# More buffers for the block sums of the experts' weights, and other numbers of pairs per stretch

## The chip, the cores and the metric

The kernel runs on one core of a Trainium2 chip. The metric is the device time of one execution in microseconds (us). TensorE (PE) multiplies matrices, VectorE (DVE) and ScalarE (ACT) work elementwise, SyncE (SP) issues nearly all transfers, and 16 DMA engines carry them out.

## The reference

Three layers follow each other on 2304 tokens (4 batches of 576) of width 512:

```python
kv = einsum('bhsd,bhse->bhde', k, v);  out = einsum('bhsd,bhde->bhse', q, kv)
x = out / sqrt(mean(out * out, -1) + 1e-6) * g_norm          # linear attention
h = x @ w_in;  x = (h * clip(h + 3, 0, 6) / 6) @ w_out       # first feed-forward, d_ff 2048
p = domain_probs / (domain_probs.sum(-1) + 1e-9)
out = sum over 4 experts e of p[:, e] * (relu(x @ w1[e]) @ w2[e])     # d_ff 1024 each
```

All is float32. The kernel gets that accuracy from pairs: an operand is split in a high part, rounded to float32r, and the low rest, and three products (high x high, high x low, low x high) stand for one.

## The kernel before

*Stages.* The attention comes first (to about 70 us). Then the first feed-forward, up to about 473 us. Then the experts, to the end.

*First feed-forward.* The tokens lie in five blocks `t` (four of 512, block 4 of 256). The 2048 hidden columns are 16 weight tiles of 128, taken in five units `u` of 1, 2, 3, 4 and 6 tiles (`UNITS1`). A step `n` is one (u, t, f); there are 80. In step n the 12 matmuls of `ff_in` (lines 360 to 362, `ph`) make a hidden tile, ACT and DVE apply the nonlinearity and split it into `gH` and `gL` (lines 373 to 377), and the 12 matmuls of `ff_out` of step n - 3 (line 395) add into four PSUM banks `po`. There are six such banks. After the last tile of a unit `ff_end` drains the four banks into `acc[t]`: ACT and DVE copy in unit 0, DVE adds later (line 413). `acc` tiles come from pool `accp`, five slots of 8 KB a partition, so block 4, half as long, fills half a slot.

*Conversion of weight tiles.* `convert(n)` turns raw 64-bit weights of tile n into `W`, in one of eight slots w0 to w7 of pool `wp`: tile n goes to w((6 + n) mod 8). It works on four buffers of 512 words a partition in pool `cvp` (tags x, a, and r with two). ACT (lines 166, 167), DVE (169 to 180) and again ACT (182, high part) and DVE (184, low part) make half 0, which `ff_in` needs, and then half 1, for `ff_out`. `load_raw` (line 152) fetches halves into `rawp`, three buffers. Conversions are paced by `pull(n)`, a tile only after the last use of the tile eight before it.

*Block sums.* The experts use a product scheme of seven instead of eight block products. It needs sums of blocks of `w1` and `w2`, which are split in high and low and put into DRAM (`dwin`, `dtw`, `dwo`) for later. This is `blocks(k, h)`: k is one of 16 pairs of hidden tiles, h is 0 for `w1` and 1 for `w2`. It takes 6 pieces: two of sums on DVE (line 676) and four calls of `keep` with an ACT copy (line 662), a DVE subtraction (line 663) and the transfers on SP (lines 666, 670, and 672 for the last two k). Each gets eight buffers `tb` from `new()`, in turn out of the four buffers of `cvp`:

```python
tag = ("x", "a", "r", "r")[turns[0] % 4]
```

A buffer can be written again when its transfer to DRAM has landed. The raw block (`rawt`, 512 KB) comes by lines 636 and 640 into `rawp`, and the next load is issued after the last piece of the one before.

*Stretches.* 24 calls of `blocks` are done within the first feed-forward, in three stretches between conversions, since both use `cvp` and `rawp`: from step 23 (after tile 9), from step 37 (after tile 13) and from step 54 (after tile 15). `BLOCKS` lists for each stretch the last tile converted, how many raw blocks are loaded in advance and the pairs; `second(n)` advances so many pieces a step.

*The start of the experts.* From step 69 on a list `ahead` of 20 jobs is worked off beside the steps: splits and differences of `acc` (`build(0)`) and the conversions `convert_in(0)`, `convert_in(1)` of the first two pairs into `win`, whose raw tiles (`load1`, line 779) lie in w6 and w7. TensorE first uses `win[0]` at line 1032, and goes on at line 885.

*Order.* Up to step 4 the order on the engines is written by hand. From there on a planner that runs when the program is built puts the instructions of each engine in order, with its own estimates of durations and the text order as priority. An engine works its list strictly in order.

Of the kernel before, what the change touches and what calls it, by code (L numbers as in the profile page):

```python
# [8 lines left out]
F32 = mybir.dt.float32  # L9
F32R = mybir.dt.float32r  # L10
# [7 lines left out]
def kernel(  # L18
# [22 lines left out]
    P = 128  # L41
    KD = DM // P
    TB = 512
# [29 lines left out]
    accp = ctx.enter_context(tc.tile_pool(name="accp", bufs=NB))  # L73
# [3 lines left out]
    wp = wst.enter_context(tc.tile_pool(name="wp", bufs=1, side="right"))  # L77
# [4 lines left out]
    cvp = early.enter_context(tc.tile_pool(name="cvp", bufs=1, side="right"))  # L82
# [7 lines left out]
    NG = CJ * 2  # L90
# [46 lines left out]
    def load_raw():  # L137
        if not todo:
            return
        nn, h = todo.pop(0)  # L140
        u, f = ftiles[nn]
        g = sum(UNITS1[:u]) + f
        r = rawp.tile([P, KD * P, 2], U32, tag="raw", name="raw")
        if h == 0:
            dst = r.rearrange("p (c f) w -> p c (f w)", c=KD)
            src = moe_w_in.bitcast(U32)[:, 2 * g * P:2 * (g + 1) * P].rearrange("(c p) f -> p c f", p=P)
        else:
            dst = r.rearrange("p (c f) w -> p c (f w)", c=2)
            src = moe_w_out.bitcast(U32)[g * P:(g + 1) * P, :].rearrange("p (c f) -> p c f", c=2)
        n = dst.shape[1] // 2  # L150
        for c in (slice(0, 2 * n),) if done[0] or len(flow) < 8 else (slice(0, n), slice(n, 2 * n)):
            paced(nc.sync.dma_start(out=dst[:, c], in_=src[:, c]))
        raw[nn, h] = r
# [189 lines left out]


    acc = {}
    gt = {}
    po_t = {}

# [53 lines left out]
    def ff_end(u, t):  # L402
        ps = po_t.pop((u, t))
        n = BLK[t][1]
        if u == 0:
            acc[t] = accp.tile([P, KD, n], F32, tag="acc", name="acc1")
        for o, p in enumerate(ps):
            if u == 0 and o < KD - 1:
                nc.scalar.activation(out=acc[t][:, o, :], in_=p, func=AF.Copy)
            elif u == 0:  # L410
                nc.vector.tensor_copy(out=acc[t][:, o, :], in_=p)
            else:
                nc.vector.tensor_tensor(out=acc[t][:, o, :], in0=p, in1=acc[t][:, o, :], op=ALU.add)  # L413
# [11 lines left out]
    def step(n):  # L425
        if n < NI:
            ff_in(*items[n])
        if n >= NB + LAG:
            for _ in ff_out(*items[n - LAG]):
                pass  # L430

        if 0 <= n - LAG + 1 < NI:
            u, t, _ = items[n - LAG + 1]
            rate = RATE[u] // (1 + (u == 3 and t == NB - 1))
            budget[0] = min(budget[0] + rate, rate)
            pull(n)
# [180 lines left out]
    TC = DM // 2  # L617
    experts = [(e, j) for e in range(E) for j in range(FP)]
    NG = len(experts) // 2
# [7 lines left out]
    def load_rawt():  # L627
        if not wanted:
            return
        k, h = wanted.pop(0)  # L630
        e, j = experts[k]
        f = 2 * j * P
        r = rawp.tile([P, 4, 2 * P], F32, tag="raw", name="rawt")
        rawt[k, h] = r
        if h:
            nc.sync.dma_start(
                out=r.rearrange("p (f c) d -> p f (c d)", f=2),
                in_=moe2_w2[e, f:f + 2 * P, :].rearrange("(f p) d -> p f d", p=P))
        else:
            nc.sync.dma_start(out=r, in_=moe2_w1[e, :, f:f + 2 * P].rearrange("(c p) f -> p c f", p=P))  # L640

    turns = [0]

    def blocks(k, h):

        r = rawt[k, h]
        last = k - 2 * NG + 2 if h else -1

        def new():
            tag = ("x", "a", "r", "r")[turns[0] % 4]  # L650
            turns[0] += 1
            return cvp.tile([P, 2, TC], F32R, tag=tag, bufs=2 if tag == "r" else 1, name="tb")

        def keep(m, src, low, n=2):
            high = new()
            low = low if low is not None else new()
            hi, lo = high[:, :n], low[:, :n]
            if src is None:
                src = lo.bitcast(F32)
            elif not h:  # L660
                hi, lo = (x.rearrange("p m (c f) -> p (m c) f", c=2) for x in (hi, lo))
            nc.scalar.activation(out=hi, in_=src, func=AF.Copy)
            nc.vector.tensor_tensor(out=lo, in0=src, in1=hi.bitcast(F32), op=ALU.subtract)  # L663
            for y, x in ((0, high), (1, low)):
                if not h:
                    nc.sync.dma_start(
                        out=dwin[k][:, y, m:m + n].rearrange("p m c f -> p m (c f)"), in_=x[:, :n].bitcast(F32))
                    continue
                c = min(n, 7 - m) if m else 1
                nc.sync.dma_start(out=dtw[k // 2][:, m:m + c, k % 2, y], in_=x[:, :c].bitcast(F32))  # L670
                if last >= 0 and m < 2:
                    nc.sync.dma_start(
                        out=dwo[last][:, int(m > 0), y].rearrange("p (c d) -> p c d", c=2), in_=x.bitcast(F32))

        def sub(out, a, b, op=ALU.subtract):
            nc.vector.tensor_tensor(out=out, in0=a, in1=b, op=op)  # L676

        odd = new()
        od = odd.bitcast(F32)
        if h:  # L680
            sub(od, r[:, 1::2], r[:, 0:2])
        else:
            q = r.rearrange("p c (i f) -> p i c f", i=2)
            a11, a12, a21, a22 = (q[:, i, 2 * c:2 * c + 2] for i in range(2) for c in range(2))
            o4 = od.rearrange("p m (c f) -> p m c f", c=2)
            sub(o4[:, 0], a21, a22, ALU.add)
            sub(o4[:, 1], o4[:, 0], a11)
        yield
        even = new()
        ev = even.bitcast(F32)  # L690
        if h:
            sub(ev[:, 0], r[:, 3], od[:, 0])
            sub(ev[:, 1], r[:, 2], ev[:, 0])
        else:
            e4 = ev.rearrange("p m (c f) -> p m c f", c=2)
            sub(e4[:, 0], a11, a21)
            sub(e4[:, 1], a12, o4[:, 1])
        yield
        keep(3, None, odd)
        yield  # L700
        keep(5, None, even)
        yield
        if h:
            keep(1, r[:, 2:4], None)
        else:
            keep(0, q[:, 0], None)
        yield
        if not h:
            keep(2, a22, None, 1)
        elif last >= 0:  # L710
            keep(0, r[:, 0:2], None)
        else:
            keep(0, r[:, 0:1], None, 1)
        rawt.pop((k, h))
        load_rawt()
        yield

    stream = []
    BLOCKS = {
        23: (9, 2, [(2, 0), (4, 0), (6, 0), (8, 0)]),  # L720
        37: (13, 2, [(k, 1) for k in range(9)] + [(10, 0)]),
        54: (15, 3, [(k, 1) for k in range(9, 2 * NG)] + [(12, 0), (14, 0), (15, 0)]),
    }

    def second(n):
        if n in BLOCKS:
            tile, deep, todo2 = BLOCKS[n]
            assert not stream and not rawt and cv[0] == tile + 1
            assert tile + 1 == len(ftiles) or todo[0] == (tile + 1, 1)
            wanted.extend(todo2)  # L730
            for _ in range(deep):
                load_rawt()
            stream.extend(x for k in todo2 for x in [blocks(*k)] * 6)
        for _ in range(5 if 23 < n < 29 or 54 < n < 68 else 6 if 37 < n < 48 else 0):
            if stream:
                next(stream.pop(0))
        if n in (28, 29, 48, 49):
            load_raw()

    N3 = start[NU1 - 1, 0] + 3 * UF[NU1 - 1]  # L740
    for n in range(NB, N3 + 1):
        step(n)
        second(n)
# [153 lines left out]
    ahead += [run(convert_in(0, sums))] * 6 + [run(convert_in(1, sums))] * 6  # L897
    for n in range(N3 + 1, NI):
        step(n)
        for _ in range(2):  # L900
            if ahead:
                ahead.pop(0)()
    for x in ahead + [first["7-"], first[7], first[3]]:
# [199 lines left out]
    for jj, i, f in order:  # L1103
        t, o = divmod(i * P, TH)
# [37 lines left out]
```

## Time and profile before

| | us |
|---|---|
| median of 3 runs | 1190.9 (1189.87 to 1192.04) |
| profiled execution, its own time | 1192.36 |
| its span, first to last instruction | 1190.5 |
| TensorE busy | 1164.2 (98%) |
| DVE busy | 871.6 (73%) |
| ACT busy | 591.1 (50%) |

Times in the trace count from the first instruction. Matmuls overlap in their pipeline, so an interval between starts tells more than a duration. The granted clock is TensorE's, as a share of 2.4 GHz.

### The profile page before, as it was taken

How to read it: one execution, taken by the hardware profiler on the slowest of the kernel's cores; microseconds unless marked ns; L12 is line 12 of the kernel's file. 1: busy time of each engine (PE TensorE's matmuls, PEld its weight loads, DVE VectorE, ACT ScalarE, POOL GpSimd, SP SyncE). 2: the span in 40 equal slices, each digit the busy share in tenths (PEclk: the TensorE clock that was granted, in tenths of full speed). 3: DMA queues.
4: the chain of work that ended last, by engine and by line, in shares of the span. 5: the costliest groups of instructions: out<-in, count | busy, mean ns of one | idle time of the engine just before them, and what ended most of it. 6: DMA issues, size and time to landing. Idle time of an engine off the chain costs nothing.

```text
span 1190.5 us, 20959 instructions
## 1 busy us (share of the span) xinstructions
PE 1164.2 (98%) x8244; PEld 1087.4 (91%) x8244; DVE 871.6 (73%) x1572; ACT 591.1 (50%) x1052; POOL 7.6 (1%) x15
## 2 busy tenths in 40 slices
PE   8999999999959999999999999999999999999998
PEld 6788888888848879999999999999999999999997
DVE  5889987976777796677777696666666866666663
ACT  5877544644454553544444454444444544444441
POOL 1100000000000000000000000000000000000000
PEclk9999999999989999999999999999999999999999
DMA  8723255467868856477777889777777897777721
GB/s 308 244 76 122 89 181 192 140 209 242 274 217 266 273 218 229 161 260 268 265 266 272 309 289 328 255 251 248 251 248 249 296 327 249 251 247 249 252 103 53
DMA packets 105686, 274.60 MB, mean 231 GB/s; under 512 B 9460, under 2 KB 56564, under 8 KB 99188
## 3 DMA queue, kind: packets, MB, share of 16 engines
q1 hardware_dynamic: 105104, 272.48, 66.2%
q8 instruction: 65, 1.06, 0.4%
q10 hardware_dynamic: 484, 0.79, 0.2%
q14 instruction: 33, 0.27, 0.1%
HBM read 207.69 MB, written 65.54 MB: 230 GB/s over the span
## 4 chain that ended last, share of the span: by engine, by line
PE 84%; DMA 7%; DVE 6%; ACT 1%; issue 1%; SPq 0%; DVEq 0%; ACTq 0%
PE slot L1011 29%; PE qa L885 15%; PE qb L885 15%; PE po L395 11%; PE ph L360 4%; PE ph L362 4%; PE ph L361 4%; DMA dtw<-tb 3%; PE slot L1106 1%; DMA vin<-in_v_dram 1%; DVE tb L663 1%; DVE tb L676 1%; DMA kin<-in_k_dram 1%; DMA dwin<-tb 1%; DMA qin<-in_q_dram 1%
## 5 line engine op out<-in xcount | busy, mean ns | idle before, releaser
L1011 PE MATMUL slot<-tt,so 128*128 128x256 f32 x2898 | 372.0, 282 | 0.0
L1011 PEld LDWEIGHTS slot<-tt,so 128*128 128x128 f32 x2898 | 365.7, 190 | 0.3 <-ACT slot L1018 0.2
L865 DVE SCALAR_TENSOR_TENSOR acc<-slot,prob,acc 128x256 f32<-128x256 f32 (+1 forms) x384 | 163.8, 482 | 112.7 <-PE slot L1011 103.8
L885 PE MATMUL qa<-xs,win 128*128 128x384 f32 x1008 | 202.4, 335 | 0.2 <-ACT qa L947 0.2
L885 PE MATMUL qb<-xs,win 128*128 128x384 f32 x1008 | 202.4, 335 | 0.0
L395 PE MATMUL po<-gH,w 128*128 128x512 f32 (+1 forms) x632 | 191.0, 368 | 1.7 <-DVE acc L413 1.6
L784 DVE TENSOR_TENSOR so<-ar,so 128x768 fp32r<-128x768 f32 x142 | 135.3, 954 | 57.3 <-ACT so L783 56.2
L885 PEld LDWEIGHTS qa<-xs,win 128*128 128x128 f32 x1008 | 173.8, 188 | 0.6 <-ACT qa L947 0.5
L885 PEld LDWEIGHTS qb<-xs,win 128*128 128x128 f32 x1008 | 172.7, 189 | 0.1
L783 ACT ACTIVATE so<-ar 128x768 fp32r<-128x768 f32 x142 | 119.4, 842 | 37.7 <-PE slot L1011 32.3
L395 PEld LDWEIGHTS po<-gH,w 128*128 128x128 f32 x632 | 115.7, 188 | 22.5 <-DVE acc L413 2.0
L360 PE MATMUL ph<-xh,w 128*128 128x512 f32 (+1 forms) x320 | 119.5, 374 | 12.8 <-ACT w L182 12.7
L361 PE MATMUL ph<-xl,w 128*128 128x512 f32 (+1 forms) x320 | 118.4, 370 | 0.0
L362 PE MATMUL ph<-xh,w 128*128 128x512 f32 (+1 forms) x320 | 118.2, 370 | 0.0
L395 PE MATMUL po<-gL,w 128*128 128x512 f32 (+1 forms) x316 | 116.4, 368 | 0.0
L943 ACT ACTIVATE ar<-cs 128x384 f32<-128x384 f32 x96 | 50.4, 525 | 113.8 <-DVE cs L972 60.7
L360 PEld LDWEIGHTS ph<-xh,w 128*128 128x128 f32 x320 | 60.7, 190 | 24.4 <-ACT w L182 13.6
L373 ACT ACTIVATE r<-ph,three 128x512 f32<-128x512 f32 (+1 forms) x80 | 51.2, 640 | 53.4 <-PE ph L362 52.4
L362 PEld LDWEIGHTS ph<-xh,w 128*128 128x128 f32 x320 | 60.5, 189 | 10.8 <-DVE w L184 0.5
L361 PEld LDWEIGHTS ph<-xl,w 128*128 128x128 f32 x320 | 60.7, 190 | 9.9
L374 DVE SCALAR_TENSOR_TENSOR r<-r,ph 128x512 f32<-128x512 f32 (+1 forms) x80 | 50.4, 631 | 25.6 <-ACT r L373 25.3
L395 PEld LDWEIGHTS po<-gL,w 128*128 128x128 f32 x316 | 59.6, 189 | 9.8 <-DVE gL L377 0.2
(142 smaller groups left out, 1162.4 us busy)
## 6 DMA issues: line engine op xcount, KB each, us to landing
tt<-dtw SPq DMA_DIRECT2D x161, 512.0 KB, 4.7
win<-dwin SPq DMA_DIRECT2D x40, 1792.0 KB, 8.0
dtw<-tb SPq DMA_DIRECT2D x96, 256.0 KB, 2.3
dwin<-win SPq DMA_DIRECT2D x8, 1792.0 KB, 9.3
rawt<-in_moe_w_dram SPq DMA_DIRECT2D x24, 512.0 KB, 3.9
dwin<-tb SPq DMA_DIRECT2D x48, 256.0 KB, 2.1
raw<-in_moe_w_in_dram SPq DMA_DIRECT2D x14, 512.0 KB, 3.9
raw<-in_moe_w_out_dram SPq DMA_DIRECT2D x14, 512.0 KB, 3.2
```

The lines of the kernel that those rows point to most:

```text
L360: nc.tensor.matmul(ph, lhsT=w[:, 0, c, :], rhs=xH[t][:, c, :], start=(c == 0), stop=False)
L361: nc.tensor.matmul(ph, lhsT=w[:, 0, c, :], rhs=xL[t][:, c, :], start=False, stop=False)
L362: nc.tensor.matmul(ph, lhsT=w[:, 1, c, :], rhs=xH[t][:, c, :], start=False, stop=(c == KD - 1))
L373: lambda: nc.scalar.activation(out=r, in_=ph, func=AF.Relu, bias=three[:, 0:1]),
L374: lambda: nc.vector.scalar_tensor_tensor(out=r, in0=r, scalar=6.0, in1=ph, op0=ALU.min, op1=ALU.mult),
L395: nc.tensor.matmul(po_t[u, t][o], lhsT=lhsT, rhs=rhs, start=(f == 0 and m == 0), stop=(f == UF[u] - 1 and m == 2))
L783: nc.scalar.activation(out=dst[0], in_=src, func=AF.Copy)
L784: nc.vector.tensor_tensor(out=dst[1], in0=src, in1=dst[0].bitcast(F32), op=ALU.subtract)
L865: nc.vector.scalar_tensor_tensor(out=acc2[i][:, c], in0=ps, scalar=pe, in1=acc2[i][:, c], op0=ALU.mult, op1=ALU.add)
L885: nc.tensor.matmul(bank, lhsT=w[:, wy, AOP[m], c], rhs=xs[m][:, xy, c], start=first and n == 0, stop=n == 5, skip_group_check=True)
L943: nc.scalar.activation(out=a[t][:, f, jj], in_=src, func=AF.Relu)
L1011: nc.tensor.matmul(dst, lhsT=o[:, sy_, jj, i * P:(i + 1) * P], rhs=t[:, jj, ty], start=fresh and m == 0 and i != 1, stop=m == 5, skip_grou ...
```

## The change

`new()` takes its buffers from a list `ring`, made anew for each stretch: the four of `cvp` as before, two that lie in the unused half of block 4's `acc` slot, and, in the first and third stretch, four in w0 and eight in w6 and w7. The stretches get 5, 8 and 11 pairs in place of 4, 10 and 10, at 6, 5 and 6 (one step) or 5 pieces a step in place of 5, 6 and 5. In the two steps after the third stretch one job of `ahead` is done a step, not two.

```diff
+    spare = []
...
         if u == 0:
-            acc[t] = accp.tile([P, KD, n], F32, tag="acc", name="acc1")
+            if n < TB:
+                both = accp.tile([P, 2, KD, n], F32, tag="acc", name="acc1")
+                acc[t] = both[:, 0]
+                spare.append(both[:, 1].rearrange("p (z m) c -> p z m c", z=2).bitcast(F32R))
+            else:
+                acc[t] = accp.tile([P, KD, n], F32, tag="acc", name="acc1")
...
         def new():
-            tag = ("x", "a", "r", "r")[turns[0] % 4]
             turns[0] += 1
-            return cvp.tile([P, 2, TC], F32R, tag=tag, bufs=2 if tag == "r" else 1, name="tb")
+            z = ring[turns[0] % len(ring)]
+            if not isinstance(z, str):
+                return z
+            return cvp.tile([P, 2, TC], F32R, tag=z, bufs=2 if z == "r" else 1, name="tb")
...
     stream = []
+    ring = []
     BLOCKS = {
-        23: (9, 2, [(2, 0), (4, 0), (6, 0), (8, 0)]),
-        37: (13, 2, [(k, 1) for k in range(9)] + [(10, 0)]),
-        54: (15, 3, [(k, 1) for k in range(9, 2 * NG)] + [(12, 0), (14, 0), (15, 0)]),
+        23: (9, 2, (0,), [(2, 0), (4, 0), (6, 0), (8, 0), (10, 0)]),
+        37: (13, 2, (), [(k, 1) for k in range(8)]),
+        54: (15, 3, (6, 7), [(k, 1) for k in range(8, 2 * NG)] + [(12, 0), (14, 0), (15, 0)]),
     }
...
-            tile, deep, todo2 = BLOCKS[n]
+            tile, deep, slots, todo2 = BLOCKS[n]
+            views = spare + [wp.tile([P, 4, 2, TC], F32R, tag=f"w{z}", name="tb") for z in slots]
+            ring[:] = ["x", "a", "r", "r"] + [v[:, z] for v in views for z in range(v.shape[1])]
...
-        for _ in range(5 if 23 < n < 29 or 54 < n < 68 else 6 if 37 < n < 48 else 0):
+        for _ in range(6 if 23 < n < 29 or n == 55 else 5 if 37 < n < 48 or 55 < n < 68 else 0):
...
-        for _ in range(2):
+        for _ in range(2 if n > N3 + 2 else 1):
             if ahead:
                 ahead.pop(0)()
```

## Rows read from the trace of the kernel before

**Rows 1.** The page, busy time, share of the span and instructions:

```profile
PE 1164.2 (98%) x8244; PEld 1087.4 (91%) x8244; DVE 871.6 (73%) x1572; ACT 591.1 (50%) x1052; POOL 7.6 (1%) x15
```

**Rows 2.** Waits of TensorE: sum in us, times, longest:

```profile
PE ph L360 <- ACT w L182: 12.7, 2, 11.2
...
PE po L395 <- DVE acc L413: 1.6, 1, 1.6
```

**Rows 3.** Timeline of TensorE: start, duration, line, idle time before it:

```profile
318.05 0.39 PE L395 MATMUL po<-gH,w 128*128 128x512 f32 x1
...
328.70 0.39 PE L395 MATMUL po<-gH,w 128*128 128x512 f32 x1
340.25 0.80 PE L360 MATMUL ph<-xh,w 128*128 128x512 f32 x1 [11.16 <-ACT w L182]
...
343.40 0.40 PE L361 MATMUL ph<-xl,w 128*128 128x512 f32 x1
...
346.29 0.50 PE L360 MATMUL ph<-xh,w 128*128 128x512 f32 x1 [1.57 <-ACT w L182]
...
434.60 0.50 PE L395 MATMUL po<-gH,w 128*128 128x512 f32 x1 [1.55 <-DVE acc L413]
```

**Rows 4.** Window behind the long wait: busy time, PEclk, DMA share, GB/s:

```profile
340.25:343.40 3.15, 3.15 (x7) 2.39 (x8) 3.04 (x7) 1.93 (x3) 0.00 (x0) 0.50 0.44 160
```

**Rows 5.** Timelines of ACT and DVE at the conversion of tile 14:

```profile
334.79 1.36 ACT L167 ACTIVATE r<-raw 128x512 uint32<-128x512 uint32 x2 [0.43 <-DMA dwin<-tb]
...
339.57 0.63 ACT L182 ACTIVATE w<-r 128x512 fp32r<-128x512 f32 x1
...
340.29 0.69 DVE L184 TENSOR_TENSOR w<-r,w 128x512 fp32r<-128x512 f32 x1
```

**Rows 6.** Windows of three stretches, `tb` alone: DVE, ACT, PEclk, DMA share, GB/s:

```profile
156.20:199.90 43.70, 15.97 (x32) 9.06 (x16) 1.00 0.57 205
235.50:335.20 99.70, 39.40 (x71) 22.85 (x40) 0.99 0.72 243
349.00:446.60 97.60, 39.88 (x73) 23.40 (x40) 1.00 0.72 249
```

**Rows 7.** Waits of DVE for transfers, 235.5 to 335.2:

```profile
DVE tb L663 <- DMA dtw<-tb: 7.4, 9, 2.5
...
DVE tb L676 <- DMA dtw<-tb: 6.0, 9, 1.2
...
DVE tb L663 <- DMA dwin<-tb: 2.3, 2, 1.5
```

**Rows 8.** Transfers issued, 235.5 to 335.2: size of one, median us to landing:

```profile
dtw<-tb SPq DMA_DIRECT2D x54, 256.0 KB, 2.4
rawt<-in_moe_w_dram SPq DMA_DIRECT2D x8, 512.0 KB, 3.9
dtw<-tb SPq DMA_DIRECT2D x18, 128.0 KB, 2.0
...
raw<-in_moe_w_dram SPq DMA_DIRECT2D x2, 512.0 KB, 5.9
```

**Rows 9.** Window of the first stretch: PE, PEld, DVE, ACT, POOL, then as above:

```profile
156.20:199.90 43.70, 43.70 (x206) 36.64 (x205) 33.49 (x64) 19.59 (x35) 0.00 (x0) 1.00 0.57 205
```

**Rows 10.** Timeline of DVE before the drain of line 413:

```profile
431.37 0.43 DVE L676 TENSOR_TENSOR tb<-rawt 128x256 f32<-128x256 f32 x1 [1.05 <-DMA dwin<-tb]
...
432.65 1.29 DVE L663 TENSOR_TENSOR tb<-tb 128x512 fp32r<-128x512 f32 x2
433.86 1.88 DVE L413 TENSOR_TENSOR acc<-po,acc 128x512 f32<-128x512 f32 x3
```

**Rows 11.** Instructions on `win`, 440 to 476: durations in ns, first and last start:

```profile
L783 ACT ACTIVATE win<-raw x4: 400/508/617, 449.5 to 451.9; 128x512 fp32r<-128x512 f32 x2, 128x256 fp32r<-128x256 f32 x2
...
L806 SPq DMA_DIRECT2D dwin<-win x2: 319/320/320, 452.5 to 457.1; - x2
...
L1032 PE MATMUL qb<-xs,win x1: 339/339/339, 467.5 to 467.5; 128*128 128x384 f32 x1
```

## The prediction

> **What bounds the kernel now.** I read the page's busy shares first, then who TensorE waited for, then TensorE's own timeline at each of those places, and last the windows and waits of the three stretches in which block sums are made. The reader is to see first that TensorE is the bound almost everywhere: 98% busy [rows 1]. So the change can only give back time in which TensorE stood still or ran slowly. Two of its waits lie where the change works: 12.7 us in two waits of line 360 for the first half of a weight tile (ACT, line 182), and 1.6 us in one wait of line 395 for a drain of PSUM (DVE, line 413) [rows 2].
>
> The timeline gives what they cost in starts of matmuls. Undisturbed, 512-column matmuls start 0.227 us apart (four groups of 12 from 318.05, the 48th at 328.70: 47 intervals in 10.65 us) [rows 3]. The next was due at 328.93 and came at 340.25: 11.32 us. The trace's wait is 0.16 us shorter, 11.16, since it counts from the end of a matmul that lasts 0.39; I add 0.16 to the two short waits as well. The seven intervals after it took 3.15 us (340.25 to 343.40) where 1.59 would do: 1.56 us. In that window the granted clock was 0.50 [rows 4], the 1.2 GHz level, after TensorE had stood idle for 11.16 us. The wait before 346.29 costs 1.57 + 0.16 = 1.73 us, the one before 434.60 costs 1.55 + 0.16 = 1.71. Sum: 11.32 + 1.56 + 1.73 + 1.71 = **16.3 us**.
>
> Why was tile 14 late? Its conversion could only begin on ACT at 334.79 and its first half was written from 339.57 to 340.20 [rows 5], because it uses the `cvp` buffers that the block sums still held: the second stretch of block sums ran from 235.5 to 335.2, ten pairs in 99.7 us, 9.97 us a pair [rows 6]. In that window block sums kept DVE busy for only 39.40 us, 3.9 us a pair [rows 6], and DVE waited 7.4 + 6.0 + 2.3 = 15.7 us for buffers still being written to DRAM [rows 7]. So the stretch is long because four buffers circulate, and the transfer that frees one lands 2.4 us after its issue [rows 8]. The first stretch takes 43.7 / 4 = 10.9 us a pair, the third 97.6 / 10 = 9.76 [rows 6].
>
> **The change part by part.** The ring becomes 4 + 2 + 4 = 10 buffers in the first stretch (two in block 4's half of `acc`, four in w0), 4 + 2 = 6 in the second, 4 + 2 + 8 = 14 in the third (w6 and w7). The 24 pairs stay 24, with the same operations and transfers: nothing is added to DVE, ACT, or the SP queue in sum. Two pairs leave the second stretch, one goes to the first and one to the third.
>
> *Rate of a pair.* With four buffers the rows have 9.97 us; that is the bound without gain. The floor is the DMA engines: a pair of the second stretch writes six transfers of 256 KB and two of 128 KB and reads 512 KB [rows 8], 2.36 MB; 243 GB/s at a share of 0.72 [rows 6] would be 337 at a full share, so 7.0 us. In between lies the stretch without DVE's waits for these transfers: (99.7 - 15.7) / 10 = 8.4 us. I take 8.4, since these waits are just what two more buffers shorten.
>
> The Trainium skill, "DMA: Bandwidth & Descriptors", section "Latency and other measured facts", speaks against that: HBM access goes from 0.2 us on average to 2 us at high load, so more writes in flight would land later. No run here shows it yet. By it, an estimate: a buffer's turn goes from 4 x 9.97 / 8 = 5.0 us to 6.8, and six buffers give 9.1 us a pair. That makes 0.7 us a pair against my value and leaves the sum as it is, but is a reason to give rival C below more than a token chance.
>
> *First stretch.* It starts at 156.2. Five pairs end between 156.2 + 5 x 7.0 = 191 and 156.2 + 5 x 10.9 = 210.8. I leave its end at 199.9, and so the second stretch's start at 235.5; in the slow bound that start moves by 10.9 us to 246.4. The fifth pair costs DVE 15.97 / 4 = 4.0 us [rows 6]. DVE has 43.7 - 33.49 = 10.2 us idle there [rows 9]: covered. Uncovered it would cost nothing on TensorE until tile 14, as there is no wait of TensorE between these stretches.
>
> *Second stretch.* Eight pairs: 235.5 + 8 x 8.4 = 302.7; bounds 291.5 (7.0) and 315.3 (9.97). In before, tile 14's first half was there 5.0 us after the stretch's end (340.2 against 335.2). So it is there at 307.7, or at 320.3 in the slow bound. TensorE wants it after four groups of line 395 that were put ahead of it (318.05 to 328.93, 10.88 us, 2.72 each) [rows 3]: at 328.93 in the order of before, at 318.05 + 2.72 = 320.8 if the planner puts only one group ahead, as in a plain step. Both are later than 307.7 and than 320.3. The stall, the slow clock behind it and the second wait go: 14.6 us. What is late next is nothing: tile 15 came with the same conversion, one step later.
>
> *Third stretch.* In before it began 349.0 - 335.2 = 13.8 us after the second, the time of the two conversions. So it begins at 316.5. Eleven pairs at 8.4 end at 408.9; at 7.0 at 393.5. The wait of line 395 before 434.60 moves with TensorE's time to 434.6 - 14.6 = 420, so no block sum is left then. In before the drain at 433.86 stood in DVE's queue behind two block operations (432.65), and ahead of those DVE had waited 1.05 us for a transfer [rows 10]. So I take this 1.71 us as gone; at 9.76 us a pair it would stay.
>
> *Moved loads.* w6 and w7 are also the home of the raw tiles of the experts' first two pairs. In before their two loads were issued within the second stretch and landed after 5.9 us [rows 8]. Now they wait on SP for the third stretch's last transfers. Behind them on SP stand only later transfers of the same conversion. The price: end of stretch + 2.4 (last landing) + 5.9 (load) + four sums of 0.43, as an operation of 256 columns takes [rows 10], and 452.5 - 449.5 = 3.0 of splitting [rows 11], 13.0 us, so `win[0]` is there at 421.9. TensorE first uses it at line 1032, 467.5 [rows 11], now 451.2. Slack: 29 us; cost nothing. The slack is gone when the stretch ends after 438.2. The slower schedule of the `ahead` pieces (one instead of two for two steps) moves two of 20 pieces by a step and lies within it.
>
> **Sum.** The profiled execution took 1192.36 us: 1192.36 - 16.3 = 1176.1. The median is 1.46 us lower, 1174.6 by the same sum. I forecast 1175.2, between the two.
>
> **The rivals.**
> *B, a short wait stays or a new one comes.* The long wait goes, but the drain's wait remains, or DVE, now without pauses, delays a drain or a half of `gH` elsewhere: 1.7 to 5 us, 1177 to 1180. For it: DVE works through the same amount in 16 us less. Against it: DVE is busy 73% of the span [rows 1], and only one wait for a drain shows even so [rows 2].
> *C, the buffers do not help.* If the planner's order or the DMA engines and not the buffers set 10.9 and 9.97 us a pair, the first stretch delays the second: 246.4 + 79.8 = 326.2, tile 14 at 331.2, a wait of 2.3 to 10.4 us. The third starts at 340.0 and ends at 447.4, `win[0]` is there at 460.4 against 451.2. Together 9 to 10 us of the gain are lost: 1184 to 1186. Against it: 15.7 us of DVE's waits are for these very transfers.
> *D, slower: the views of one tile count as one buffer.* If a write to one quarter of w6 waited for the landing of the transfer from another quarter, 7 of the 14 entries would wait for their neighbour: four of a pair's eight buffers, each for a copy of 0.63, a subtraction of 0.69 [rows 5] and a landing of 2.4 us, 3.7 us, so 14.9 us a pair. The third stretch would end at 316.5 + 164 = 480.5 and `win[0]` come at 493.5: 42 us late, 1217 us. Slower than before from 12.8 us a pair on (end at 456.9). Against it: line 360 started at 340.25 on one half of tile 14 while line 184 began to write the other only at 340.29 [rows 3, 5], so halves of a tile are followed one by one.
> *E, nothing changes.* Tile 14's lateness has a cause that I don't see and moves along: 1190.9. Against it: its ACT instructions followed the last block sum at once.
>
> **Chances.** Forecast (all waits gone) 0.71, B 0.12, C 0.08, D 0.05, E 0.04. Faster by over 0.2% (about what a measurement of this kernel can tell from no change) is the first three: 0.91; same 0.04; slower 0.05. The forecast's low end is 1174.6 less 1.1 us of spread between runs and 0.7 for small ripples behind the waits, 1172.8; with B the range goes to 1181 and holds 0.83.
>
> **What would show it.** Right: no wait of line 360 for line 182 after 100 us; granted clock 1.00 from 325 to 350; second stretch of eight pairs ending before 316; tile 14's first half before 320; line 1032 near 451. Each step is wrong by itself if: a pair still takes about 10 us (rate); `tb` operations wait for transfers out of the same tile (D); line 1032 or 885 waits for `win` (moved loads); line 395 still waits for line 413 (B). The prediction is wrong as a whole if TensorE waits again at tile 14 or at the start of the experts.

## The result and the profile after

The changed kernel takes 1176.24 us (median of 4 runs, 1175.23 to 1177.54), the kernel before beside it 1191.47: ratio 0.9867, interval 0.9839 to 0.9896. A second time, beside other kernels, it took 1175.26 us against 1191.02 (0.9864, 0.985 to 0.9879). The forecast was 1175.2. The profiled execution took 1175.23, its span is 1173.4 (before 1190.5).

Line numbers have shifted: 360 is now 361, 395 is 396, 413 is 419, 662 and 663 are 670 and 671, 676 is 684, 783 and 784 are 794 and 795, 1032 is 1043; 182 stays.

First the page: busy times, and the granted clock in 40 slices, all nines.

```profile
PE 1160.9 (99%) x8244; PEld 1086.0 (93%) x8244; DVE 867.7 (74%) x1572; ACT 587.0 (50%) x1052; POOL 7.6 (1%) x15
...
PEclk9999999999999999999999999999999999999999
```

Next the waits of TensorE (sum, times, longest), the answers to [rows 2]. The 12.7 us for line 182 are gone, and so are the 1.6 us for the drain at 434.60. The 0.2 us that are left for a drain belong to an earlier one, at 302.13 in TensorE's timeline, where the kernel before showed no wait.

```profile
PE kvp L249 <- DMA vin<-in_v_dram: 3.8, 4, 1.6
...
PE po L396 <- DVE acc L419: 0.2, 1, 0.2
```

```profile
302.13 0.39 PE L396 MATMUL po<-gH,w 128*128 128x256 f32 x1 [0.19 <-DVE acc L419]
```

TensorE's timeline at the two places, the answer to [rows 3]: the first use of tile 14 now follows 0.23 us after the matmul ahead of it, and so does line 361 at 418.52 behind the group that the drain had held up. No idle time stands in brackets.

```profile
320.37 0.39 PE L396 MATMUL po<-gH,w 128*128 128x512 f32 x1
320.60 0.39 PE L361 MATMUL ph<-xh,w 128*128 128x512 f32 x1
...
418.29 0.39 PE L396 MATMUL po<-gH,w 128*128 128x512 f32 x1
418.52 0.39 PE L361 MATMUL ph<-xh,w 128*128 128x512 f32 x1
```

Where the 17.05 us of the span went, by TensorE's starts in the two traces (the gains are taken before rounding):

| place | before | after | gained so far |
|---|---|---|---|
| first matmul of step 49 | 299.77 | 299.26 | 0.50 |
| of step 53, just before tile 14 | 315.30 | 315.13 | 0.17 |
| of step 57, tile 14 in use | 351.96 | 336.92 | 15.05 |
| of step 72, behind the drain | 435.39 | 418.52 | 16.88 |
| line 1032, now 1043 | 467.47 | 450.57 | 16.90 |
| end | 1190.48 | 1173.43 | 17.05 |

So 14.88 us came at tile 14 and 1.83 at the drain; the first 0.50 lie in the attention, where nothing was changed, 0.33 were lost between steps 49 and 53 around the new short wait at 302.13, and the last 0.17 came behind the drain.

The windows of the three stretches (`tb` alone: DVE, ACT, clock, DMA share, GB/s), the answer to [rows 6], and one of all engines while tile 14 is taken up, the answer to [rows 4]. They miss the work in the two buffers in `acc`, which go by that name.

```profile
155.00:188.60 33.60, 17.80 (x37) 9.70 (x18) 1.00 0.83 291
228.20:294.30 66.10, 27.57 (x51) 14.86 (x26) 1.00 0.85 282
311.30:390.60 79.30, 40.43 (x77) 21.91 (x41) 1.00 0.97 337
...
320.60:336.90 16.30, 16.30 (x73) 13.51 (x72) 15.15 (x30) 8.63 (x17) 0.00 (x0) 1.00 1.02 331
```

A pair takes 33.6 / 5 = 6.7, 66.1 / 8 = 8.3 and 79.3 / 11 = 7.2 us, where it took 10.9, 9.97 and 9.76. DVE's waits in the second stretch, the answer to [rows 7], show 1.6 + 1.5 + 1.1 us for transfers, and the 5.7 us for ACT are partly hidden waits for transfers too:

```profile
DVE tb L671 <- ACT tb L670: 5.7, 2, 2.9
DVE acc L684 <- DMA dtw<-acc: 1.6, 1, 1.6
DVE acc L671 <- DMA dtw<-acc: 1.5, 2, 1.3
...
DVE tb L684 <- DMA dtw<-tb: 1.1, 1, 1.1
```

The transfers of the second stretch, then of the third (count, size, median us to landing), the answer to [rows 8]: what landed after 2.4 us takes 3.9 with six buffers in turn and 5.3 with fourteen.

```profile
dtw<-tb SPq DMA_DIRECT2D x32, 256.0 KB, 3.9
...
dtw<-tb SPq DMA_DIRECT2D x42, 256.0 KB, 5.3
```

ACT's timeline shows the first half of tile 14 written by 305.11, 15.5 us before TensorE takes it; in the kernel before it was written at 340.20, while TensorE stood waiting for it [rows 3, 5]. The list of instructions on `win` shows the last split, that of `win[1]`, at 415.2 against a first use of `win[0]` at 450.6 [rows 11].

```profile
304.49 0.62 ACT L182 ACTIVATE w<-r 128x512 fp32r<-128x512 f32 x1
```

```profile
L795 DVE TENSOR_TENSOR win<-sums,win x4: 676/678/680, 406.5 to 415.2; 128x512 fp32r<-128x512 f32 x4
...
L1043 PE MATMUL qb<-xs,win x1: 339/339/339, 450.6 to 450.6; 128*128 128x384 f32 x1
```

### The profile page after: what moved, and what is told of

Read it like the earlier page. It is cut to its first block, busy times and chain, and to the rows that moved or that the text cites. A ratio compares the mean times of both kernels' runs of the same rounds, so it can differ in the third digit from the quotient of the medians.

```text
span 1173.4 us, 20890 instructions
## 1 busy us (share of the span) xinstructions
PE 1160.9 (99%) x8244; PEld 1086.0 (93%) x8244; DVE 867.7 (74%) x1572; ACT 587.0 (50%) x1052; POOL 7.6 (1%) x15
## 4 chain that ended last, share of the span: by engine, by line
PE 88%; DMA 5%; DVE 4%; ACT 1%; issue 1%; SPq 0%; DVEq 0%; ACTq 0%
PE slot L1022 29%; PE qa L896 15%; PE qb L896 15%; PE po L396 13%; PE ph L361 5%; PE ph L363 4%; PE ph L362 4%; DMA dtw<-tb 2%; PE slot L1117 1%; DMA vin<-in_v_dram 1%; DMA kin<-in_k_dram 1%; DMA qin<-in_q_dram 1%; DVE tb L671 1%; DVE xl L318 1%; DMA dtw<-acc 1%
## 5 line engine op out<-in xcount | busy, mean ns | idle before, releaser
L794 ACT ACTIVATE so<-ar 128x768 fp32r<-128x768 f32 x142 | 119.4, 842 | 38.9 <-PE slot L1022 33.6
L361 PEld LDWEIGHTS ph<-xh,w 128*128 128x128 f32 x320 | 60.3, 188 | 10.8 <-DVE r L375 0.4
```

Of the source, the lines that this page charges most:

```text
L361: nc.tensor.matmul(ph, lhsT=w[:, 0, c, :], rhs=xH[t][:, c, :], start=(c == 0), stop=False)
L794: nc.scalar.activation(out=dst[0], in_=src, func=AF.Copy)
```

## The experiments

The theory: TensorE is the bound, and all that the stretches can cost is (a) tile 14's first half too late and (b) a block operation in DVE's queue ahead of a drain. More buffers give the gain because they make (a) early. The question was which buffers, and whether the new numbers of pairs do anything by themselves.

All kernels in one table. Buffers and pairs are for the three stretches. "Second" is the stretch's first and last block operation, "tile 14" is when its first half was written and when TensorE first used it, "rest" is TensorE's time from the first matmul of step 8 to the end; these three come from the one profiled execution of each.

| kernel | buffers | pairs | median us | ratio (interval) | second | tile 14 | rest |
|---|---|---|---|---|---|---|---|
| before | 4/4/4 | 4/10/10 | 1190.7 to 1191.5 | 1 | 235.5–335.2 | 340.2, 340.25 | 1097.3 |
| after | 10/6/14 | 5/8/11 | 1176.24 | 0.9867 (0.9839–0.9896) | 228.2–294.3 | 305.1, 320.6 | 1080.7 |
| after again | 10/6/14 | 5/8/11 | 1175.26 | 0.9864 (0.985–0.9879) | 229.0–292.4 | 303.8, 320.9 | 1080.3 |
| ring alone | 10/6/14 | 4/10/10 | 1176.60 | 0.9882 (0.9868–0.9897) | 223.9–305.0 | 308.4, 321.5 | 1081.4 |
| pairs alone | 4/4/4 | 5/8/11 | 1181.11 | 0.9915 (0.99–0.993) | 243.9–320.8 | 327.95, 328.0 | 1087.1 |
| old `ahead` | 10/6/14 | 5/8/11 | 1176.16 | 0.9876 (0.9862–0.989) | 228.2–291.5 | 303.0, 320.2 | 1080.5 |
| six everywhere | 6/6/6 | 5/8/11 | 1181.66 | 0.9924 (0.9912–0.9936) | 238.9–305.9 | 312.0, 327.2 | 1085.9 |
| no w6, w7 | 10/6/6 | 5/8/11 | 1175.23 | 0.986 (0.9846–0.9873) | 228.2–294.0 | 304.9, 320.3 | 1080.5 |
| no w0 | 6/6/14 | 5/8/11 | 1182.31 | 0.9913 (0.9899–0.9928) | 240.3–307.9 | 314.1, 329.6 | 1086.9 |
| twelve in second | 10/6/14 | 5/12/7 | 1179.51 | 0.9894 (0.9879–0.9908) | 228.2–324.7 | 327.72, 327.77 | 1084.6 |
| six with seven | 6/6/6 | 5/7/12 | 1181.10 | 0.9914 (0.9899–0.9928) | 237.5–297.1 | 308.3, 325.0 | 1084.1 |
| w0 alone | 8/4/4 | 5/8/11 | 1175.20 | 0.9865 (0.9848–0.9881) | 229.7–308.1 | 315.1, 320.0 | 1080.9 |
| 10/6/6, old pairs | 10/6/6 | 4/10/10 | 1176.63 | 0.9875 (0.986–0.9889) | 224.0–304.8 | 308.4, 321.4 | 1081.6 |
| six with six | 6/6/6 | 5/6/13 | 1178.09 | 0.989 (0.9875–0.9905) | 238.4–289.8 | 305.1, 322.1 | 1081.0 |

**Ring alone**: the pairs, pieces a step and `ahead` of before, the new ring (the edits to the pieces and to `ahead` are left out here).

```diff
-        23: (9, 2, (0,), [(2, 0), (4, 0), (6, 0), (8, 0), (10, 0)]),
-        37: (13, 2, (), [(k, 1) for k in range(8)]),
-        54: (15, 3, (6, 7), [(k, 1) for k in range(8, 2 * NG)] + ...
+        23: (9, 2, (0,), [(2, 0), (4, 0), (6, 0), (8, 0)]),
+        37: (13, 2, (), [(k, 1) for k in range(9)] + [(10, 0)]),
+        54: (15, 3, (6, 7), [(k, 1) for k in range(9, 2 * NG)] + ...
```

> The larger ring alone: 10, 6 and 14 buffers, but 4, 10 and 10 pairs at the rates of before, and two ahead jobs a step. My theory (the end of the second stretch decides, and buffers set its rate): about 8.3 us a pair as in the changed kernel, second stretch from about 228 to 311, first half of tile 14 about 316 to 318, before TensorE wants it at 320.6; no wait of line 361 for line 182, about 1176 to 1177 us. Rival (the number of pairs in the second stretch is what cured it, the buffers do little): about 9.97 us a pair, the wait of some 11 us is still there, 1188 to 1191 us.

Measured 1176.60, no wait at tile 14. The ring needs no new pairs.

**Pairs alone**: the kernel before with 5, 8 and 11 pairs and the pieces a step that go with them, four buffers.

> The other numbers of pairs alone: 5, 8 and 11 pairs at 6, 5 and 6 or 5 pieces a step, with the four buffers of before. My theory (case C of the prediction with its cause put in by hand): 10.9 us a pair in the first stretch, about 10 in the second, second stretch from about 246 to 326, first half of tile 14 at about 331, a wait of 2 to 10 us at tile 14, third stretch until about 447, win[0] about 460: 1183 to 1187 us. Rival (pairs do it): no wait at tile 14, 1176 us.

Measured 1181.11, under the expected 1183 to 1187: the pairs alone win 9.6 of the 15.2 to 15.8 us, as tile 14 comes at 327.95. TensorE's timeline in this kernel (line numbers of the kernel before) and the window behind the wait:

```profile
328.00 0.79 PE L360 MATMUL ph<-xh,w 128*128 128x512 f32 x1 [3.17 <-ACT w L182]
```

```profile
328.00:333.60 5.60, 5.60 (x13) 4.44 (x14) 4.07 (x8) 1.92 (x3) 0.00 (x0) 0.50 0.48 176
```

The reader is to see that 3.17 us of standing still cost more than themselves: from 328.00 to 333.71 thirteen intervals took 5.71 us where 13 x 0.227 = 2.95 would do, at a granted clock of 0.50. Steps 53 to 57 took 28.21 us against 21.79 in the kernel after, 6.42 more. This wait is the rest of the one of before, and the theory's (a).

**Old `ahead`**: two jobs a step throughout.

```diff
-        for _ in range(2 if n > N3 + 2 else 1):
+        for _ in range(2):
```

> The changed kernel with two ahead jobs a step from step 69 on, as before. My theory: this part hides in slack, since win[0] is there long before line 1043 wants it: the same as the changed kernel within 0.1%, 1176 us. Rival (the slower schedule keeps DVE free for the drain of line 419 and is what removed the 1.7 us wait of line 396 for it): that wait is back, about 1178 us.

Measured 1176.16: this part of the change is worth nothing here.

**Six everywhere**: neither w0 nor w6 and w7.

```diff
-        23: (9, 2, (0,), [(2, 0), ...
+        23: (9, 2, (), [(2, 0), ...
-        54: (15, 3, (6, 7), [(k, 1) ...
+        54: (15, 3, (), [(k, 1) ...
```

> The changed kernel without w0, w6 and w7: six buffers in all three stretches, 5, 8 and 11 pairs. My theory: 8.3 to 8.5 us a pair in the first and third stretch too, the third ends at about 405 instead of 390, long before line 1043: no wait of TensorE comes back, the same as the changed kernel, 1176 to 1177 us. Rival (the free weight tiles are needed): first stretch near 11 us a pair, tile 14 late again by some us, or a drain of line 419 late in the third stretch, 1178 us or more.

A miss: 1181.66. Tile 14 came in time, as expected, but the second stretch now ended at 305.9, and (b) happened. ACT's, DVE's and TensorE's timelines, and a window behind:

```profile
305.03 0.42 ACT L670 ACTIVATE tb<-rawt 128x256 fp32r<-128x256 f32 x1 [3.48 <-DMA dtw<-tb]
```

```profile
305.48 0.42 DVE L671 TENSOR_TENSOR tb<-rawt,tb 128x256 fp32r<-128x256 f32 x1 [3.40 <-ACT tb L670]
305.82 0.68 DVE L419 TENSOR_TENSOR acc<-po,acc 128x512 f32<-128x512 f32 x1
```

```profile
306.56 0.41 PE L396 MATMUL po<-gH,w 128*128 128x256 f32 x1 [2.74 <-DVE acc L419]
```

```profile
308.00:310.00 2.00, 2.00 (x7) 1.62 (x6) 1.97 (x6) 1.54 (x4) 0.00 (x0) 0.50 0.75 240
```

Read from the top: the last piece of the stretch waits 3.48 us on ACT for a buffer whose transfer has not landed; DVE waits for that piece; the drain stands behind it in DVE's queue; TensorE waits for the drain, and runs at half clock afterwards. From step 49 to 53 the kernel lost 20.21 - 15.87 = 4.34 us. In the kernel after the same two waits are there, 2.92 us on ACT and 2.91 on DVE, but they end at 293.8. The drain comes at 300.46; what stands ahead of it there is the conversion of tile 14, as DVE's timeline shows, and this costs TensorE the 0.19 us at 302.13. In after again steps 49 to 53 take 15.41 us, without a wait.

```profile
299.79 0.43 DVE L172 TENSOR_SCALAR x<-x 128x512 uint32<-128x512 uint32 x1
...
300.46 0.68 DVE L419 TENSOR_TENSOR acc<-po,acc 128x512 f32<-128x512 f32 x1
```

**No w6 and w7**, and **no w0**: one of the two lines above each.

> The changed kernel without w6 and w7: 10, 6 and 6 buffers. My theory after the run with six everywhere (what hurt there was the first stretch at 10.1 us a pair, which put the end of the second stretch from 294 to 306, onto the drain of step 49): the first two stretches stay as in the changed kernel, the third runs at 8.6 us a pair and ends near 407, no wait: 1176 to 1177 us. Rival (the third stretch needs its 14 buffers): about 1181 us, with a wait in the third stretch or at the start of the experts.

> The changed kernel without w0: 6, 6 and 14 buffers. My theory: first stretch at 10 us a pair, second from about 239 to 306, its last pieces wait for a landing ahead of the drain of line 419, TensorE waits 2 to 3 us there and runs slowly for some matmuls after: 1181 us, as with six everywhere. Rival (w0 is of no use): 1176 us.

Measured 1175.23 and 1182.31, each within 1.4 us of what was expected. The eight buffers in w6 and w7 are worth nothing that these runs tell; the four in w0 are worth all that six everywhere lacks. In the kernel without w0 the same chain as above made TensorE wait 2.73 us for the drain at 308.58, after 0.99 us for an earlier one at 289.50. Not all of the loss is this chain: six everywhere and no w0 reach step 8, before any block sum, at 94.3 and 95.5 us, the kernel after at 92.7 and 93.5, which no run explains.

**Twelve in second**: 5, 12 and 7 pairs, eight pieces a step in the second stretch.

```diff
-        37: (13, 2, (), [(k, 1) for k in range(8)]),
+        37: (13, 2, (), [(k, 1) for k in range(12)]),
-        54: (15, 3, (6, 7), [(k, 1) for k in range(8, 2 * NG)] + ...
+        54: (15, 3, (6, 7), [(k, 1) for k in range(12, 2 * NG)] + ...
```

> The changed kernel with 5, 12 and 7 pairs, 8 pieces a step in the second stretch. My theory (end of the second stretch = start + pairs x 8.2 us, tile 14's first half some 5 us behind it): from 228 to 327, tile 14 at about 332; TensorE wants it at 320.6, or at 328.9 if the planner puts more groups of line 396 ahead: a wait of 3 to 11 us and 1.5 to 3 us of slow clock, 1181 to 1189 us. Rival (with more buffers the stretch no longer holds up tile 14): no wait, 1176 us.

Measured 1179.51. The stretch ended at 324.7, and tile 14's first half was written at 327.72; the wait is (a) again, in TensorE's timeline, with a window at half clock behind it:

```profile
327.77 0.80 PE L361 MATMUL ph<-xh,w 128*128 128x512 f32 x1 [2.20 <-ACT w L182]
```

```profile
328.00:330.00 2.00, 2.00 (x5) 1.59 (x6) 1.77 (x3) 0.96 (x2) 0.00 (x0) 0.50 0.91 349
```

So more buffers don't help if the stretch gets pairs enough to reach the same date: the date counts, not the buffers. Steps 53 to 57 took 4.75 us more than in the kernel after. The time lies under the expected 1181 to 1189, as 12 pairs went at 8.0 us each and conversion came only 3.0 us behind the stretch.

**Six with seven**: six buffers, 5, 7 and 12 pairs, to end the second stretch ahead of the drain. The slots go as in six everywhere, pair 7 moves to the third stretch, and that one has six pieces a step; the diff shows one of these lines.

```diff
...
-        37: (13, 2, (), [(k, 1) for k in range(8)]),
+        37: (13, 2, (), [(k, 1) for k in range(7)]),
...
```

> Six buffers in all stretches as before, but 5, 7 and 12 pairs. My theory (with six everywhere only the place of the second stretch's end hurt, 305.9, in front of the drain of step 49): one pair less ends it at about 297, the last pieces' wait for a landing then has no drain behind it that TensorE needs at once, 1176 to 1178 us. Rival (six buffers in the first or third stretch cost time by themselves): again about 1181 us.

A second miss: 1181.10. The stretch ended at 297.1, before the drain, but now the conversion of tile 14 stood there. DVE's timeline, TensorE's, and a window behind:

```profile
300.74 0.69 DVE L176 SCALAR_TENSOR_TENSOR a<-raw,x 128x512 uint32<-128x512 uint32 x1
301.46 0.69 DVE L180 CUSTOM_DVE_ANT_0 r<-r,a 128x1024 uint16<-128x1024 uint16 x1
...
302.98 0.41 DVE L375 SCALAR_TENSOR_TENSOR r<-r,ph 128x256 f32<-128x256 f32 x1
303.31 0.68 DVE L419 TENSOR_TENSOR acc<-po,acc 128x512 f32<-128x512 f32 x1
```

```profile
304.04 0.39 PE L396 MATMUL po<-gH,w 128*128 128x256 f32 x1 [1.42 <-DVE acc L419]
...
304.98 0.53 PE L396 MATMUL po<-gH,w 128*128 128x256 f32 x1 [0.30 <-DVE acc L419]
```

```profile
306.00:308.00 2.00, 2.00 (x6) 1.52 (x6) 1.88 (x5) 1.25 (x3) 0.00 (x0) 0.50 0.03 9
```

It is (b) with another operation in front: steps 49 to 53 cost 19.24 - 15.87 = 3.37 us. The rival gave the same time, but these 3.37 us lie at the drain. Another 1.05 us of the profiled execution lie ahead of step 8 (93.73 against 92.68), before any block sum, and no run explains them.

**w0 alone**: no spare half of `acc` and no w6 and w7, so eight buffers in the first stretch and four as before in the others.

```diff
-            views = spare + [wp.tile(...) for z in slots]
+            views = [wp.tile(...) for z in slots]
-        54: (15, 3, (6, 7), ...
+        54: (15, 3, (), ...
```

> Eight buffers in the first stretch (w0), four in the second and third: no spare half of acc, no w6 and w7; 5, 8 and 11 pairs. If w0 counts because the first stretch ends early and lets the second begin near 228: the first ends by 191, the second runs 228 + 8 x 9.6 = 305, tile 14's first half is there near 312 against a want at 321, no wait of line 361 for line 182; but the second stretch's last pieces then stand in DVE's queue at the drain near 301 to 306, as with six buffers everywhere, so a wait of line 396 for line 419 of 1.4 to 2.8 us with half clock behind it: 1178 to 1182. Rival, the two halves of acc in the second stretch are what counts: tile 14 comes after 325 and line 361 waits again: 1182 to 1186.

A third miss, to the good side: 1175.20, with no wait of line 396 above 0.2. Tile 14 came near the 312 that was said (315.1), but the drain was not held up: DVE's timeline has its operations from 297.96 on between pieces that did not wait.

```profile
299.83 0.68 DVE L684 TENSOR_TENSOR tb<-rawt 128x512 f32<-128x512 f32 x1
300.43 0.69 DVE L419 TENSOR_TENSOR acc<-po,acc 128x512 f32<-128x512 f32 x1
301.03 0.42 DVE L684 TENSOR_TENSOR tb<-rawt,tb 128x256 f32<-128x256 f32 x1
```

The second stretch is as slow as before, 78.4 / 8 = 9.8 us a pair, and its transfers land as they did before (window of `tb`, then transfers of that window):

```profile
229.70:308.10 78.40, 31.31 (x56) 18.38 (x32) 1.00 0.69 236
```

```profile
dtw<-tb SPq DMA_DIRECT2D x48, 256.0 KB, 2.5
```

So the whole gain is to be had with four more buffers in one stretch and five pairs in it.

**10/6/6 with the pairs of before**, and with its pieces a step and `ahead`, as a check on a smaller ring with the old pairs:

> Ten, six and six buffers with the pairs, pieces and ahead schedule of before (4, 10, 10). Theory: w0 and the spare half are all of the gain. The first stretch ends near 183, the second runs from 224 to 305, tile 14's first half is there near 308, no wait; third stretch from 322 at 8.4 a pair ends near 406, win[0] after 419 against 450: 1175 to 1177. Rival, the buffers in w6 and w7 are needed with these pairs: the third stretch ends at 322 + 98 = 420 or later, and the wait of line 396 for the drain near 418 comes back: 1177 to 1179.

Measured 1176.63, as the theory. One wait of 0.3 us for the drain is left.

**Six with six**: 5, 6 and 13 pairs, to bring the stretch and the conversion behind it ahead of the drain; otherwise as six with seven.

```diff
...
-        37: (13, 2, (), [(k, 1) for k in range(8)]),
+        37: (13, 2, (), [(k, 1) for k in range(6)]),
...
```

> Six buffers in all three stretches with 5, 6 and 13 pairs (six everywhere with 5, 8 and 11 took 1181.7, with 5, 7 and 12 1181.1). Theory: what cost 5 us there was the place where the second stretch ended: its last pieces, or the conversion behind them, stood ahead of the drain of line 419 near 301 to 306. Six pairs end near 239 + 6 x 8.4 = 289, and conversion is through by 300: no wait of line 396 above 0.5 us before 320, clock 1.0, 1176 to 1178. Rival, six buffers in the first stretch cost time elsewhere (1 to 3 us more in the attention stage, or the third stretch's 13 pairs, to 305 + 13 x 8.6 = 417, delay the drain near 418): 1179 to 1182.

Measured 1178.09, at the edge between the theory and its rival. From step 8 to the end it takes 1081.0 us, as the kernel after does (1080.3 and 1080.7): the waits for the drain are gone with the place where the stretch ends. What it is slower by lies ahead of step 8, as the rival had it, which it reaches at 94.5 us (after: 92.7 and 93.5). The other three kernels with six buffers in the first stretch reach it at 93.7 to 95.5, all other changed kernels at 92.5 to 93.5. The order of instructions up to there is the same in all of them, so what makes this 1 to 2 us is open.

**After again** is the comparison for these three:

> The changed kernel once more, beside the kernels above on the same chip. If buffers in w6 and w7 are worth nothing, ten, six and six stay within 1.2 us of it: 1175.2 to 1177.5.

Measured 1175.26. No version beats the changed kernel; 10/6/6 with the new pairs (no w6, w7) and w0 alone match it with less.

## Why the prediction was right, point by point

*The sum.* Forecast 16.3 us; the span lost 17.05. Tile 14: 11.32 + 1.56 + 1.73 = 14.61 against 14.88 measured. Drain: 1.71 against 1.83. The rest is 0.50 of the attention stage and 0.17 behind the drain, less 0.33 around the new wait, which I had put at nothing. By the medians the gain is smaller, 15.2 and 15.8 us.

*Rate of a pair.* 8.4 against 8.3 in the second stretch. For the others it was too slow: 6.7 and 7.2. The third stretch moved 337 GB/s at a share of 0.97, what I had worked out for a full share. The first is not faster than the floor of 7.0: its window moved 33.6 x 291 = 9.8 MB where five pairs make 11.8, so part of their transfers lies outside it. Nor do two more buffers help everywhere. In the first stretch a pair takes 10.7 us with four buffers (pairs alone), 10.0 to 10.2 with six, 8.1 with eight (w0 alone) and 6.7 with ten; why six do so little there no run shows.

The prediction named a rule of the Trainium skill, "DMA: Bandwidth & Descriptors", section "Latency and other measured facts", that access to HBM slows under load. By that rule the landings should lengthen. In the second and third stretch the landings did lengthen: 2.5 us with four buffers in turn (w0 alone), 3.9 with six, 5.3 with fourteen; no run tells slower access from standing in line behind other transfers. In the first stretch it was the other way round, as the transfers of six everywhere and then of the kernel after show (from 155 to 207 us): 3.9 us with six buffers, 3.0 with ten.

```profile
dwin<-tb SPq DMA_DIRECT2D x20, 256.0 KB, 3.9
...
dwin<-tb SPq DMA_DIRECT2D x24, 256.0 KB, 3.0
```

The longer landings did not take the gain back: a buffer's turn in the second stretch became 6 x 8.3 / 8 = 6.2 us, not 6.8.

*First stretch.* Here I left a gain out. I let it end at 199.9 and the second begin at 235.5; they were 188.6 and 228.2. So the second stretch, though it had about the length that I gave it, ended at 294.3, not 302.7. Tile 14's first half was written at 305.1, near my 307.7, but by luck: it came 10.8 us behind the stretch, not 5.0, and this took back most of the 8.4. In the kernels of the table it comes 3.0 (twelve in second) to 15.3 us (six with six) behind. In all kernels of the table the second stretch begins 32 to 41 us after the first ends, so a shorter first stretch moves it; w0 alone lives on that.

*Second stretch.* Tile 14 was wanted at 320.6, one group ahead of it, as 320.8 said. Right; but "six buffers shorten the second stretch" is not what is needed. w0 alone keeps 9.8 us a pair there and loses nothing, since the start moved from 235.5 to 229.7 and two pairs had left.

*Drain.* The size was right, but not my condition that the wait would stay at 9.76 us a pair. In pairs alone (9.6 us a pair, block sums until 444) and in w0 alone (9.5, until 431) block sums were still running at this drain, and neither shows the wait. In pairs alone even the operations ahead of the drain are those of [rows 10], in the same order from the one on that waited 1.05 us for a transfer there; this wait is missing. DVE's timeline in pairs alone (line numbers of the kernel before):

```profile
421.92 1.28 DVE L663 TENSOR_TENSOR tb<-tb 128x512 fp32r<-128x512 f32 x2
423.13 1.88 DVE L413 TENSOR_TENSOR acc<-po,acc 128x512 f32<-128x512 f32 x3
```

So neither the rate nor the kind of operation decides, but when DVE gets to the drain; that the 1.05 us made the difference is read from the two timelines and was not tried. In the change no block sum is left there, as forecast. The drain near 301 to 308 is another such place, which I did not name.

*Moved loads.* `win[0]` was forecast for 421.9; it was complete when its transfer was issued, at 408.8 (`win[1]` at 415.8), and it is used at 450.6. From the end of the stretch that is 18.2 us, not the 13.0 of the sum, which the earlier end of the stretch made up for. Hidden, and w6 and w7 were not needed at all.

*Rivals.* B's mechanism is real and was priced well: 3.4 to 4.7 us in six everywhere, no w0 and six with seven; the change misses it narrowly. Its own drain already waits 0.19 us behind the conversion of tile 14, and in six with seven a stretch that ended 2.8 us later (297.1 against 294.3) lost 3.37 us. C fell with the rates. D fell: a pair took 7.2 us, not 14.9. These are DVE's waits from 311.3 to 390.6, and none is for a transfer; ACT waited 3.1 us there for writes and 1.1 us for a load.

```profile
DVE r L375 <- ACT r L374: 7.7, 6, 2.2
DVE acc L419 <- PE po L396: 2.1, 1, 2.1
DVE gL L378 <- ACT gH L377: 1.0, 3, 0.4
DVE tb L671 <- ACT tb L670: 0.8, 1, 0.8
```

## What to carry to other kernels

When the bound engine waits for a late result, look for the date that the result must meet, and count what stands ahead of it in the queues: three quite different edits met it here (the new ring with the old pairs, four buffers more in the first stretch with the new pairs, six buffers with a shorter second stretch). A stretch of background work that ends just ahead of a drain can cost about a third of what was won; look at where it ends, not only at how long it is. Add such buffers one place at a time: of the fourteen added in three places, four did the work, together with the new pairs.

## What the runs showed of the hardware

- A short wait of TensorE was followed by half clock in some places and not in others. Behind waits of 2.20, 2.73, 2.74 and 3.17 us, and behind 1.42 and 0.30 close together, the granted clock fell to 0.50. Behind the waits of 1.57 and 1.55 us in the kernel before it did not, as these windows of it show:

```profile
346.29:348.00 1.71, 1.71 (x7) 1.24 (x8) 1.71 (x4) 0.63 (x1) 0.00 (x0) 1.00 0.52 190
...
434.60:436.00 1.40, 1.40 (x6) 1.18 (x7) 1.40 (x4) 0.46 (x1) 0.00 (x0) 1.00 1.02 383
```

  So a wait can cost about twice itself: 3.37 us were lost for 1.72 of waiting (six with seven), 4.75 for 2.20 (twelve in second), 6.42 for 3.17 (pairs alone). In six everywhere it was less, 4.34 for 2.74. What decides is open.
- Writes of 256 KB to DRAM took 2.5, 3.9 and 5.3 us to land with four, six and fourteen buffers in turn (second stretch of w0 alone, second and third of the kernel after), while the throughput of the stretch rose from 236 to 282 and 337 GB/s. In the first stretch the order is another, 3.9 us with six buffers and 3.0 with ten, so the number of buffers alone does not set it.
